# A spectral MLP on one core: ten of twelve mixing units in three float32r passes, and the activation table loaded in the inverse

## The chip, the cores and the metric

One Trainium2 chip, one NeuronCore of it. A program is timed in device microseconds on that core. The engines are TensorE (PE; PEld is its weight load), VectorE (DVE), ScalarE (ACT), GpSimd (POOL) and SyncE (SP), which issues most of the DMAs here. Each engine runs its own queue in order and waits on semaphores of the others.

## The reference

x has 2 sequences of 3008 rows and 256 columns, all in float32.

```python
X = np.fft.rfft(x, axis=1)
Yr = Xr @ w_r - Xi @ w_i + b_r          # w_r, w_i: 256 x 256
Yi = Xr @ w_i + Xi @ w_r + b_i
Yr = np.sign(Yr) * np.maximum(np.abs(Yr) - 0.01, 0)      # Yi the same way
x = np.fft.irfft(Yr + 1j * Yi, n=3008, axis=1)           # 6016 rows of 256
h = x @ w_in1;  x = (h / (1 + np.exp(-1.702 * h))) @ w_out1   # 256 -> 2048 -> 256
h = x @ w_in2;  x = (h / (1 + np.exp(-h))) @ w_out2
```

## The kernel before

The work runs in stages. **Forward:** the real Fourier transform as matrix products: rows of x are folded (sums and differences of rows that share a cosine or a sine), multiplied with cosine and sine matrices in 16 groups, and copied from PSUM (`psf`) by ACT into tiles `xt[b, p, j, cs]` of 128x512, which hold spectrum columns as the contraction's rows (L384). **Mixing:** 12 units `(b, p, j)`; each multiplies the cosine and sine parts of 128 frequencies with the complex weight, adds the bias, shrinks and folds. **Inverse:** 16 steps `(q, b, t)` of products with the inverse matrices into `psi`; ACT copies the first two steps of a `(q, b)` into `rt` (L569), DVE adds and subtracts the other two (`ac`, `rt`, L590 and L591), and sums of these go to `yt` (L607, L611). **MLP:** two layers, six blocks of up to 1024 tokens each, eight pairs of hidden chunks per block, in float32r: an operand is split into a high part (rounded to float32r) and a low part (the rest), and a product is three passes, high by high, high by low, low by high (`passes`, `prod`, `out_mm`).

A mixing unit (`mid_mm`, `mid_post`, `mid_fold`) has two PSUM banks, from the pools `ps0` and `ps1` in turn (four banks each, so a bank comes back two units of the same pool later). PE runs 8 matmuls in float32 and one float32r matmul with the bias. The trace records a float32 matmul as two instructions of 128x512. Then ACT copies the first bank to `us` (L482); DVE makes sum and difference with the second bank, `sd` (L484 to L486); ACT applies Relu (L490), DVE clips (L491): `th`; DVE and POOL fold `th` into tiles `f` (L503, L509, L510), the inverse's stationary operands. The `f` tiles take the places of `xt` tiles that are read out.

Beside the stages runs the conversion of the MLP's weights (float64, loaded as raw words): `tick` takes a weight a step further. ACT takes an Abs of the high words (`cv_c`, L165), DVE assembles the float32 value from the bits in five ops (L170 to L174), an accumulating DMA issued by POOL adds the halves (`cv_a <- cv_c`, L227), DVE makes four small sums for an in-weight (`tmp`, L202 to L205), and ACT and POOL split the result into high part (L99) and low part (L100), tiles `wi` and `wo`. The next weight's load waits until the single `raw` buffer is free, that is for L174. In-weights 4 and 5 live in the pool `wib0`, opened at the start of the mixing.

What sets the order: in the mixing only SP's queue keeps the order of the code (`region('mid')` with 'SP'); a scheduler orders PE, ACT, DVE and POOL. In the inverse PE's order is that of the code. In the MLP it is the code's from the second pair on. ACT's table of functions is loaded where a function needs another set; `preload_act_table` would load it at inverse step `pre`, which is 17, and there are 16 steps, so the load stands before the first gate of the MLP (L717).

Of the kernel before, what the change touches and what calls it, by code (L numbers as in the profile page):

```python
# [8 lines left out]

F32 = mybir.dt.float32  # L10
CFG = {'lv0': 'V', 'lv': 'VVVVVPVVVVVP', 'dd0': 'VPVVPPPPPVVP', 'dd': 'VVVVVVVVVVPV', 'ths': 'VVVVPV', 'thf': 'VVVP', 'ivf': 'VVVPVVVV', 'cva': 'P', 'pol': 'PPPP', 'pil': 'P', 'mvl': 'PVVP', 'xl': 'V', 'xse': 'V', 'gl': 'VPPPPPPP', 'tf': [6, 9, 12], 'tm': [2, 6, 10], 'ti': [1, 4, 7, 10], 'kb': [0, 1, 1, 1, 1, 1, 1, 0], 'kr': [0, 1, 0, 1, 0, 1, 1, 0], 'fa': 3, 'xp': [2, 4, 4, 5], 'xq': [1, 4, 1], 'xs': 4, 'xi': [11, 12, 13, 15], 'xsi': 9, 'ca': 4, 'tl': True, 'fwd': 'Pool,SP', 'rest0': 'all', 'rest1': 'all', 'last1': 'all', 'inv': 'PE', 'mid': 'SP', 'last0': 'all', 'thm': 'A', 'gl0': 'PVPVVVPV', 'gl2': 'PPPPPPPP', 'gl3': 'PPPPPPPV', 'xl0': 'V', 'xl1': 'V', 'pre': 17, 'pre2': 0, 'yd': 6, 'lvb': 6, 'mlp': 'none', 'pr': 'VVVP', 'pf': 'PV', 'eo': '0000', 'ddb': 6, 'mlp1': 'all', 'mlp2': 'all'}
NUM = dict(tf=[5, 9, 13], tm=[1, 3, 5, 7, 9, 11], ti=[0, 2, 4, 6, 8, 10, 12, 14, 14, 15, 15], kb=[2] * 8, kr=1, fa=3, fe=2, pm=0, nf=4, lvb=6, ddb=8, ivb=1, eob=2, fsb=6, f1=3, f2=0, fm=[7, 8, 9], fi=[1, 1, 2, 2], pre=13, pre2=1, yd=3, psh=0, ie=[12], xp=[1, 3, 4, 5], xq=[1, 2, 2], xs=5, nw=4, xi=[14, 14, 15, 15], xsi=13, rw=2, ca=4, cc=2, tb=1, tmn=1)

DEF = dict(pr="V", pf="V", lv0="V", lv="VPP", dd0="VVVVVP", dd="VPV", mpl="PV", ths="VP", thf="VVPP", fsl="VP", ivf="PPVV", cva="P", pol="P", pil="P", mvl="V", xl="PPVVPPP", xl0="PPVVPPP", xl1="PPVVPPP", xse="VP", gl="P", gl0="P", gl2="P", gl3="P", wcl="V", thc="V", thm="V")
F32R = mybir.dt.float32r
U32 = mybir.dt.uint32
AF = mybir.ActivationFunctionType
ALU = mybir.AluOpType

B, S, D, FF = 2, 3008, 256, 2048  # L20
HALF = S // 2
P = 128
# [4 lines left out]
NPR = NFC // 2  # L27
# [24 lines left out]
def r32(ap):  # L52
    return ap.bitcast(F32)
# [3 lines left out]
def spectral_mlp_kernel(ctx, tc, xin, mfwd, minv, wc, bias, w_in1, w_out1, w_in2, w_out2, outT):  # L57
    nc = tc.nc
# [27 lines left out]
    m_p = opened("m", "left", 4)  # L86
    wia_p = opened("wia", "left", NPR // 2)
# [182 lines left out]
    raws, lvs, xs = {}, {}, {}  # L270
# [60 lines left out]
    xt = {}  # L331
# [90 lines left out]
    for g, (q, b, t) in enumerate(groups):  # L422
# [30 lines left out]
    mids = [(b, p, j) for b in range(B) for p in range(2) for j in range(NJ)]  # L453
# [352 lines left out]
    for at, (l, i, p) in enumerate(seq):  # L806
        if (l, i, p) in ((0, 0, 1), (0, 0, 2)):
            region(f'mlp{p}')
        if (i, p) == (1, 0):
            region(f'rest{l}')  # L810
        if (i, p) == (last, 0):
            region(f'last{l}')
        nxt = (l, i + 1) if i < last else (1, 0)
        more = p == NPR - 1 and (l, i) != (1, last)
        k = rate(at)

        def hook(h):
            if more:
                if h in (1, 2):
                    for x in ((0,), (1, 2))[h - 1]:  # L820
                        xprep(*nxt, x)
                if h == 3:
                    xprep(*nxt, 3, 1)
                if h == 4:
                    xprep(*nxt, 3, 2)
            if p == 0:
                for x in {1: (4,), 3: (6, 5)}.get(h, ()):
                    xprep(l, i, x)
            if h == 1 and p == NPR - 2 and (l, i) != (1, last):
# [164 lines left out]
```

## Time and profile before

| | us |
|---|---|
| Median of 3 runs (1190.44 to 1191.27) | 1191.0 |
| The profiled execution | 1191.14 |
| Its span, first to last instruction | 1189.4 |
| Mixing on PE, first matmul to the inverse's first | 66.92 to 152.12 |
| Inverse on PE, to the MLP's first | 152.12 to 207.67 |
| Activation table loads on ACT, three in the kernel, each | 1.28 |

Busy time is the time in which an engine has an instruction running. A group of rows in a timeline has the start, the length and the number of merged instructions; in brackets stands how long the engine idled before them and who released it. Lengths of neighbours overlap a little on PE and ACT, so the distance between starts is the pace. The granted clock of PE is 1.00 in every stage.

### The profile page before, as it was taken

To read this page: it belongs to the slowest core of one execution; us is meant where nothing else is said; L and a number is where in the kernel's file an instruction comes from. 1 tells how busy PE (TensorE), PEld (TensorE's weight loads), DVE (VectorE), ACT (ScalarE), POOL (GpSimd) and SP (SyncE) were. 2 spreads that over 40 slices of the span, in tenths; PEclk is the share of its full clock that TensorE was granted. 3 is DMA by queue.
4 is the path that set the end of the run, shared out by engine and by line. 5 is a ranking of instruction groups with operands and counts; after the bars stand their busy time and mean duration, and the time that the engine had idled before them with its cause. 6 is when DMAs were issued, how large, how long until landed. Compare 5 with 4: busy or idle time off the path is not lost.

```text
span 1189.4 us, 14160 instructions
## 1 busy us (share of the span) xinstructions
PE 1170.6 (98%) x4940; PEld 923.2 (78%) x4940; DVE 628.5 (53%) x969; ACT 740.8 (62%) x1398; POOL 480.3 (40%) x399
## 2 busy tenths in 40 slices
PE   7999999999999999999999999999999999999998
PEld 4744476778888888888888978878888888888897
DVE  7758868666556557465554553352442623523422
ACT  2343431678667667667677786666666766766755
POOL 2333231345443434444445755433333433433333
PEclk9999999999999999999999999999999999999999
DMA  7653102131121121221120200000000000000000
GB/s 273 201 167 80 26 1 54 38 74 49 36 60 48 53 71 36 54 72 36 36 80 9 68 13 27 1 36 1 1 36 1 4 33 1 36 1 1 36 1 31
DMA packets 30441, 55.95 MB, mean 47 GB/s; under 512 B 2721, under 2 KB 11937, under 8 KB 30370
## 3 DMA queue, kind: packets, MB, share of 16 engines
q1 hardware_dynamic: 25730, 46.66, 11.6%
q0 software_dynamic: 4640, 8.39, 4.1%
q8 instruction: 39, 0.64, 0.2%
q14 instruction: 32, 0.26, 0.1%
HBM read 36.29 MB, written 10.35 MB: 39 GB/s over the span
## 4 chain that ended last, share of the span: by engine, by line
PE 71%; ACT 5%; DVE 2%; issue 2%; DMA 0%; POOL 0%; DVEq 0%; ACTq 0%; POOLq 0%
PE o L686 38%; PE x L714 33%; ACT yt L717 2%; ACT g L719 1%; ACT x L637 1%; ACT yt L733 1%; DVE x L640 0%; DVE yt L735 0%; DVE yt L756 0%; DVE yt L690 0%; ACT yt L750 0%; DMA cv_a<-cv_c 0%; ACT yt L748 0%; ACT yt L690 0%; ACT wi L99 0%
## 5 line engine op out<-in xcount | busy, mean ns | idle before, releaser
L724 POOL TENSOR_TENSOR g<-yt,g 128x512 fp32r<-128x512 f32 (+1 forms) x282 | 361.0, 1293 | 537.7 <-PE x L714 357.7
L686 PE MATMUL o<-g,wo 128*128 128x512 f32 (+1 forms) x2304 | 560.4, 385 | 2.0 <-POOL g L724 1.1
L714 PE MATMUL x<-x,wi 128*128 128x512 f32 (+1 forms) x2016 | 500.8, 387 | 5.2 <-ACT yt L750 2.0
L686 PEld LDWEIGHTS o<-g,wo 128*128 128x128 f32 x2304 | 432.4, 188 | 84.2 <-POOL g L724 1.8
L714 PEld LDWEIGHTS x<-x,wi 128*128 128x128 f32 x2016 | 376.2, 188 | 84.7 <-ACT yt L733 5.3
L717 ACT ACTIVATE yt<-yt 128x512 f32<-128x512 f32 (+1 forms) x288 | 179.1, 622 | 254.8 <-DVE yt L756 207.7
L719 ACT CAST g<-yt 128x512 fp32r<-128x512 f32 (+1 forms) x384 | 234.3, 612 | 11.8
L756 DVE TENSOR_TENSOR yt<-yt,x 128x512 f32<-128x512 f32 (+1 forms) x96 | 64.7, 674 | 211.8 <-PE x L714 211.3
L735 DVE TENSOR_TENSOR yt<-yt,x 128x512 f32<-128x512 f32 (+1 forms) x96 | 64.8, 675 | 169.8 <-ACT yt L733 168.8
L724 DVE TENSOR_TENSOR g<-yt,g 128x512 fp32r<-128x512 f32 (+1 forms) x102 | 72.6, 712 | 77.8 <-ACT g L719 76.7
L472 PE MATMUL psm<-wc_s,xt 128*128 128x512 f32 x192 | 84.5, 592 | 0.0
L472 PEld LDWEIGHTS psm<-wc_s,xt 128*128 128x128 f32 x192 | 36.5, 190 | 43.4 <-issue 41.6
L640 DVE TENSOR_TENSOR x<-yt,x 128x512 fp32r<-128x512 f32 (+1 forms) x48 | 49.9, 1041 | 35.9 <-ACT x L637 35.9
L344 PE MATMUL psf<-m,xf 128*128 128x376 f32 (+2 forms) x208 | 59.5, 448 | 7.5 <-DVE xf L303 7.5
L759 DVE TENSOR_TENSOR yt<-yt,x 128x512 f32<-128x512 f32 (+1 forms) x96 | 64.7, 674 | 0.0
L733 ACT COPY yt<-x 128x512 f32<-128x512 f32 (+1 forms) x96 | 54.9, 572 | 9.4 <-issue 6.8
L344 PEld LDWEIGHTS psf<-m,xf 128*128 128x128 f32 x208 | 38.3, 195 | 28.1 <-DVE xf L303 9.3
L717 ACT ACTIVATE yt<-x 128x512 f32<-128x512 f32 (+1 forms) x96 | 56.1, 584 | 2.1 <-PE x L714 2.1
L750 ACT COPY yt<-x 128x512 f32<-128x512 f32 (+1 forms) x96 | 55.8, 581 | 0.8 <-PE x L714 0.8
L748 ACT COPY yt<-x 128x512 f32<-128x512 f32 (+1 forms) x96 | 54.9, 572 | 0.8 <-PE x L714 0.8
L344 PE MATMUL psi<-m,f 128*128 128x376 f32 (+3 forms) x192 | 54.7, 440 | 0.0
L344 PEld LDWEIGHTS psi<-m,f 128*128 128x128 f32 x192 | 35.3, 190 | 18.5 <-issue 0.5
(81 smaller groups left out, 651.8 us busy)
## 6 DMA issues: line engine op xcount, KB each, us to landing
raw<-in_wi SPq DMA_DIRECT2D x32, 256.0 KB, 3.0
cv_a<-cv_c POOLq DMA_DIRECT2D x32, 256.0 KB, 3.3
raw<-in_wo SPq DMA_DIRECT2D x16, 512.0 KB, 3.5
raw<-in_x SPq DMA_DIRECT2D x12, 512.0 KB, 5.1
out_t<-yt SPq DMA_DIRECT2D x20, 256.0 KB, 2.3
m<-in_mf SPq DMA_DIRECT2D x4, 564.0 KB, 6.2
m<-in_mi SPq DMA_DIRECT2D x4, 564.0 KB, 10.0
w_in<-cv_a SPq DMA_DIRECT2D x8, 256.0 KB, 2.0
```

What stands on the lines that cost most here:

```text
L344: nc.tensor.matmul(ps, hi[:, c : c + P], m[:, k, :w], start=i == 0, stop=i == last)
L472: nc.tensor.matmul(t, x[xi][:, mm], wc_s[:, mm, off : off + 2 * D], start=(n == 0), stop=(n == 3 and grp == 1))
L686: nc.tensor.matmul(acc[h, mm], st, mv, start=first and k == 0, stop=last and k == 2)
L714: nc.tensor.matmul(ps, st, mv, start=first and m == 0, stop=m == 2, skip_group_check=True)
L717: nc.scalar.activation(g, g if src is None else src, func)
L719: nc.scalar.copy(gh, g)
L724: eng.tensor_sub(gl, g, r32(gh))
L733: nc.scalar.copy(y1, X)
L735: nc.vector.tensor_add(y1, y1, Y)
L750: nc.scalar.copy(y3, X)
L756: nc.vector.tensor_add(y2, y2, X)
L759: nc.vector.tensor_add(y3, y3, Z)
```

## The change

Units 2 to 11 of the mixing (`n32` is 2) run in float32r. The weight `wc_s` is split once into `wh` (an ACT copy) and `wl` (a DVE subtract). For each of these units, and each of its two `xt` tiles, `xsplit` makes a high part `hi` by an ACT copy, and a low part in two steps: ACT writes -x rounded to float32r into `lo`, and an accumulating DMA issued by POOL adds x to it. Six buffers each for `hi` and `lo` (`nhb`) hold three units. Units 2, 3 and 4 are split before the loop, unit u+3 after the matmuls of unit u. Each of the 8 float32 matmuls becomes three float32r passes. The pool `wib0` is opened only after the mixing, in the place of the new tiles. `pre` becomes 14, so that the table for the first layer's gate is loaded in the inverse. In the settings `n32`, `nhb` and `xa` are new (`xa` is read nowhere).

```diff
@@ place_in
-        wp = wia_p if p < NPR // 2 else wib_a if p < 6 else wib_b[0]
+        wp = wia_p if p < NPR // 2 else wib_p[p // 6]
@@ the mixing
-    wib_a = opened("wib0", "left", 2)
     mid_p = opened("mid", "right", 2)
     ft = {}
+    wh_p = opened("wh", "left")
+    nh_p = opened("nh", "left", N('nhb'))
+    wh = wh_p.tile([P, 2, 3 * D], F32R, name="wh")
+    wl = wh_p.tile([P, 2, 3 * D], F32R, name="wl")
+    nc.scalar.copy(wh, wc_s)
+    nc.vector.tensor_sub(wl, wc_s, r32(wh))
+    xsp = {}
+
+    def xsplit(i):
+        if not N('n32') <= i < len(mids):
+            return
+        b, p, j = mids[i]
+        for cs in range(2):
+            x = xt[b, p, j, cs].rearrange("p q m c -> p (q m c)")
+            hi = nh_p.tile([P, 512], F32R, tag="hi", name="xh")
+            lo = nh_p.tile([P, 512], F32R, tag="lo", name="xl")
+            nc.scalar.mul(lo, x, -1.0)
+            nc.gpsimd.dma_start(out=lo, in_=x, accum_op=ALU.add)
+            nc.scalar.copy(hi, x)
+            xsp[b, p, j, cs] = [t[:, :].rearrange("p (q m c) -> p q m c", q=2, m=2) for t in (hi, lo)]
...
-                    nc.tensor.matmul(t, x[xi][:, mm], wc_s[:, mm, off : off + 2 * D], start=(n == 0), stop=(n == 3 and grp == 1))
+                    w = slice(off, off + 2 * D)
+                    if hl is None:
+                        nc.tensor.matmul(t, x[xi][:, mm], wc_s[:, mm, w], start=(n == 0), stop=(n == 3 and grp == 1))
+                    else:
+                        for k, (st, mv) in enumerate(passes(hl[xi][0][:, mm], hl[xi][1][:, mm], wh[:, mm, w], wl[:, mm, w])):
+                            nc.tensor.matmul(t, st, mv, start=n == 0 and k == 0, stop=n == 3 and grp == 1 and k == 2)
...
+    for i in range(N('n32') + 3):
+        xsplit(i)
     for i in range(len(mids)):
         ps = mid_mm(i)
+        if i >= N('n32'):
+            xsplit(i + 3)
...
-    closed("mid", "wc")
+    closed("mid", "wc", "nh", "wh")
+    wib_p.append(opened("wib0", "left", 2))
```

The scheduler's order moves with it. On ACT, at units 1 to 3 of the mixing: `us` and `th` belong to the units in turn, `xh` and `xl` to a unit three further on, `wi` are the weights' splits. Before:

```order
L482 COPY us<-psm 128x512
L165 ACTIVATE cv_c<-raw_866 128x512
L99 CAST wi_1074<-cv_a 128x384
L490 ACTIVATE th<-sd,neglam 128x512 x2
L482 COPY us<-psm 128x512
L99 CAST wi_1074<-tmp 128x512
L490 ACTIVATE th<-sd,neglam 128x512 x2
```

And now, from the same copy of unit 1 (raw_1033 is the same weight as raw_866 there):

```order
L507 COPY us<-psm 128x512
L515 ACTIVATE th<-sd,neglam 128x512 x2
L507 COPY us<-psm 128x512
L165 ACTIVATE cv_c<-raw_1033 128x512
L478 CAST xh<-xt_106 128x512
L476 ACTIVATE xl<-xt_106 128x512
L478 CAST xh<-xt_107 128x512
L476 ACTIVATE xl<-xt_107 128x512
L515 ACTIVATE th<-sd,neglam 128x512 x2
L507 COPY us<-psm 128x512
```

The split of unit 5 (xt_106, xt_107) stands behind the weight's Abs, and the casts of in-weight 4 (wi_1074) have left this place for the inverse.

On DVE, from the last unit's `sd` to the inverse's first `ac`. Before:

```order
L486 TENSOR_TENSOR sd<-psm,us 128x256
L491 SCALAR_TENSOR_TENSOR th<-sd,th 128x512 x2
L503 TENSOR_TENSOR f_1038<-th 128x512
L590 TENSOR_TENSOR ac<-rt,psi 128x377
L591 TENSOR_TENSOR rt<-rt,psi 128x377
```

And now:

```order
L511 TENSOR_TENSOR sd<-psm,us 128x256
L172 SCALAR_TENSOR_TENSOR cv_a<-raw_1243,cv_c 128x512
L516 SCALAR_TENSOR_TENSOR th<-sd,th 128x512
L173 TENSOR_SCALAR cv_c<-cv_a 128x512
L516 SCALAR_TENSOR_TENSOR th<-sd,th 128x512
L202 TENSOR_TENSOR tmp<-cv_a 128x128
L203 TENSOR_TENSOR tmp<-cv_a 128x128
L174 SCALAR_TENSOR_TENSOR cv_c<-raw_1243,cv_c 128x512
L528 TENSOR_TENSOR f_1305<-th 128x512
L204 TENSOR_TENSOR tmp<-tmp,cv_a 128x128
L205 TENSOR_TENSOR tmp<-cv_a,tmp 128x128
L170 TENSOR_SCALAR cv_c<-cv_c 128x512
```

Conversions that were done within the mixing (L172 to L174, L202 to L205, and the next weight's from L170 on) now stand between the last unit and the inverse's first sums, and three more of them among these.

## Rows read from the trace of the kernel before

**Rows 1.** Page, part 1: busy us, share of the span, instructions
```profile
PE 1170.6 (98%) x4940; PEld 923.2 (78%) x4940; DVE 628.5 (53%) x969; ACT 740.8 (62%) x1398; POOL 480.3 (40%) x399
```

**Rows 2.** The stages in windows: PE, PEld, DVE, ACT, POOL busy, PEclk, DMA share, GB/s
```profile
67.00:152.00 85.00, 85.00 (x205) 38.67 (x204) 63.27 (x117) 31.38 (x60) 26.32 (x20) 1.00 0.29 85
152.00:208.00 56.00, 56.00 (x210) 37.65 (x209) 43.84 (x66) 14.17 (x29) 13.26 (x9) 1.00 0.11 29
208.00:250.00 42.00, 39.36 (x166) 30.24 (x165) 28.29 (x44) 28.38 (x51) 15.87 (x13) 1.00 0.20 50
```

**Rows 3.** PE timeline over mixing, inverse and first MLP group: start us, length us, instruction
```profile
66.92 3.60 PE L472 MATMUL psm<-wc_s,xt 128*128 128x512 f32 x8
...
70.59 7.03 PE L472 MATMUL psm<-wc_s,xt 128*128 128x512 f32 x16
...
77.69 7.03 PE L472 MATMUL psm<-wc_s,xt 128*128 128x512 f32 x16
...
152.12 8.44 PE L344 MATMUL psi<-m,f 128*128 128x378 f32 x28
...
207.67 6.25 PE L714 MATMUL x<-x,wi 128*128 128x512 f32 x24
214.86 0.50 PE L686 MATMUL o<-g,wo 128*128 128x512 f32 x1 [0.94 <-ACT g L719]
```

**Rows 4.** A 60 us window in the MLP, PE alone
```profile
360.00:420.00 60.00, 59.80 (x264) 1.00 0.19 49
```

**Rows 5.** ACT timeline, from before the mixing to the first MLP group
```profile
58.02 1.04 ACT L322 COPY wc_s<-wc_f 128x1024 f32<-128x1024 f32 x1 [2.78 <-DMA wc_f<-in_wc]
...
74.02 0.59 ACT L384 COPY xt<-psf 128x128 f32<-128x128 f32 x3
...
91.63 0.67 ACT L165 ACTIVATE cv_c<-raw 128x512 f32<-128x512 f32 x1 [4.67 <-DMA raw<-in_wi]
...
168.81 1.14 ACT L637 CAST x<-yt 128x512 fp32r<-128x512 f32 x2 [8.38 <-DVE yt L607]
...
189.32 0.62 ACT L99 CAST wo<-cv_a 128x512 fp32r<-128x512 f32 x1 [0.79 <-DMA cv_a<-cv_c]
189.85 1.59 ACT L569 COPY rt<-psi 128x376 f32<-128x376 f32 x4
...
208.89 0.59 ACT L733 COPY yt<-x 128x512 f32<-128x512 f32 x1 [6.78 <-issue]
...
212.23 1.28 ACT L717 ACT_TABLE_LOAD   x1
```

**Rows 6.** DVE timeline, mixing and inverse
```profile
87.28 0.68 DVE L174 SCALAR_TENSOR_TENSOR cv_c<-raw,cv_c 128x512 f32<-128x512 uint32 x1
...
161.30 0.55 DVE L590 TENSOR_TENSOR ac<-rt,psi 128x377 f32<-128x377 f32 x1 [5.34 <-PE psi L344]
...
190.26 1.38 DVE L173 TENSOR_SCALAR cv_c<-cv_a 128x512 uint32<-128x512 uint32 x1
...
202.54 0.55 DVE L590 TENSOR_TENSOR ac<-rt,psi 128x376 f32<-128x376 f32 x1 [2.14 <-PE psi L344]
```

**Rows 7.** POOL timeline, mixing and inverse
```profile
113.62 1.71 POOL L503 TENSOR_TENSOR f<-th 128x512 f32<-128x512 f32 x1 [1.48 <-DVE th L491]
...
190.03 1.33 POOL L100 TENSOR_TENSOR wo<-cv_a,wo 128x512 fp32r<-128x512 f32 x1 [4.31 <-ACT wo L99]
```

**Rows 8.** Page, part 3 (queue of accumulating DMAs) and part 6 (issue to landing)
```profile
q0 software_dynamic: 4640, 8.39, 4.1%
...
cv_a<-cv_c POOLq DMA_DIRECT2D x32, 256.0 KB, 3.3
```

**Rows 9.** The tile cv_a, 55 to 215 us: min/median/max
```profile
L227 POOL DMA_DIRECT2D cv_a<-cv_c x9: 849/870/877, 54.5 to 193.2; - x9
...
DMA to landing us min/median/max: 3.3/4.4/7.9
```

**Rows 10.** DMA issues from 70 to 80 us, while matrices are loaded
```profile
cv_a<-cv_c POOLq DMA_DIRECT2D x1, 256.0 KB, 6.6
```

More of the change, by code (lines that the diff above doesn't have):

```diff
@@ L10 @@
 F32 = mybir.dt.float32
-CFG = {'lv0': 'V', 'lv': 'VVVVVPVVVVVP', 'dd0': 'VPVVPPPPPVVP', 'dd': 'VVVVVVVVVVPV', 'ths': 'VVVVPV', 'thf': 'VVVP', 'ivf': 'VVVPVVVV', 'cva': 'P', 'pol': 'PPPP', 'pil': 'P', 'mvl': 'PVVP', 'xl': 'V', 'xse': 'V', 'gl': 'VPPPPPPP', 'tf': [6, 9, 12], 'tm': [2, 6, 10], 'ti': [1, 4, 7, 10], 'kb': [0, 1, 1, 1, 1, 1, 1, 0], 'kr': [0, 1, 0, 1, 0, 1, 1, 0], 'fa': 3, 'xp': [2, 4, 4, 5], 'xq': [1, 4, 1], 'xs': 4, 'xi': [11, 12, 13, 15], 'xsi': 9, 'ca': 4, 'tl': True, 'fwd': 'Pool,SP', 'rest0': 'all', 'rest1': 'all', 'last1': 'all', 'inv': 'PE', 'mid': 'SP', 'last0': 'all', 'thm': 'A', 'gl0': 'PVPVVVPV', 'gl2': 'PPPPPPPP', 'gl3': 'PPPPPPPV', 'xl0': 'V', 'xl1': 'V', 'pre': 17, 'pre2': 0, 'yd': 6, 'lvb': 6, 'mlp': 'none', 'pr': 'VVVP', 'pf': 'PV', 'eo': '0000', 'ddb': 6, 'mlp1': 'all', 'mlp2': 'all'}
@@ L12 @@
-NUM = dict(tf=[5, 9, 13], tm=[1, 3, 5, 7, 9, 11], ti=[0, 2, 4, 6, 8, 10, 12, 14, 14, 15, 15], kb=[2] * 8, kr=1, fa=3, fe=2, pm=0, nf=4, lvb=6, ddb=8, ivb=1, eob=2, fsb=6, f1=3, f2=0, fm=[7, 8, 9], fi=[1, 1, 2, 2], pre=13, pre2=1, yd=3, psh=0, ie=[12], xp=[1, 3, 4, 5], xq=[1, 2, 2], xs=5, nw=4, xi=[14, 14, 15, 15], xsi=13, rw=2, ca=4, cc=2, tb=1, tmn=1)
+CFG = {'lv0': 'V', 'lv': 'VVVVVPVVVVVP', 'dd0': 'VPVVPPPPPVVP', 'dd': 'VVVVVVVVVVPV', 'ths': 'VVVVPV', 'thf': 'VVVP', 'ivf': 'VVVPVVVV', 'cva': 'P', 'pol': 'PPPP', 'pil': 'P', 'mvl': 'PVVP', 'xl': 'V', 'xse': 'V', 'gl': 'VPPPPPPP', 'tf': [6, 9, 12], 'tm': [2, 6, 10], 'ti': [1, 4, 7, 10], 'kb': [0, 1, 1, 1, 1, 1, 1, 0], 'kr': [0, 1, 0, 1, 0, 1, 1, 0], 'fa': 3, 'xp': [2, 4, 4, 5], 'xq': [1, 4, 1], 'xs': 4, 'xi': [11, 12, 13, 15], 'xsi': 9, 'ca': 4, 'tl': True, 'fwd': 'Pool,SP', 'rest0': 'all', 'rest1': 'all', 'last1': 'all', 'inv': 'PE', 'mid': 'SP', 'last0': 'all', 'thm': 'A', 'gl0': 'PVPVVVPV', 'gl2': 'PPPPPPPP', 'gl3': 'PPPPPPPV', 'xl0': 'V', 'xl1': 'V', 'pre': 14, 'pre2': 0, 'yd': 6, 'lvb': 6, 'mlp': 'none', 'pr': 'VVVP', 'pf': 'PV', 'eo': '0000', 'n32': 2, 'xa': 4, 'nhb': 6, 'ddb': 6, 'mlp1': 'all', 'mlp2': 'all'}
@@ L14 @@
+NUM = dict(n32=2, nhb=6, tf=[5, 9, 13], tm=[1, 3, 5, 7, 9, 11], ti=[0, 2, 4, 6, 8, 10, 12, 14, 14, 15, 15], kb=[2] * 8, kr=1, fa=3, fe=2, pm=0, nf=4, lvb=6, ddb=8, ivb=1, eob=2, fsb=6, f1=3, f2=0, fm=[7, 8, 9], fi=[1, 1, 2, 2], pre=13, pre2=1, yd=3, psh=0, ie=[12], xp=[1, 3, 4, 5], xq=[1, 2, 2], xs=5, nw=4, xi=[14, 14, 15, 15], xsi=13, rw=2, ca=4, cc=2, tb=1, tmn=1)
 DEF = dict(pr="V", pf="V", lv0="V", lv="VPP", dd0="VVVVVP", dd="VPV", mpl="PV", ths="VP", thf="VVPP", fsl="VP", ivf="PPVV", cva="P", pol="P", pil="P", mvl="V", xl="PPVVPPP", xl0="PPVVPPP", xl1="PPVVPPP", xse="VP", gl="P", gl0="P", gl2="P", gl3="P", wcl="V", thc="V", thm="V")
@@ L209, in place_in @@
         )
-    wib_b = []
+    wib_p = []
     spare = []
@@ L464, in mid_mm @@
         x = [xt[b, p, j, cs][:, q] for cs in range(2) for q in range(2)]
+        hl = [[v[:, q] for v in xsp[b, p, j, cs]] for cs in range(2) for q in range(2)] if (b, p, j, 0) in xsp else None
         ps = []
@@ L852, in spectral_mlp_kernel @@
             closed("iv")
-            wib_b.append(opened("wib1", "left", 2))
+            wib_p.append(opened("wib1", "left", 2))
         if N('pre2') and (l, i, p) == (0, last, NPR - 1):
```

## The prediction

> **What bounds the kernel now.** I read the page's shares first: TensorE (PE) is busy 98% of the span [rows 1], so only a stage's PE time, or a wait that ends at PE, is worth anything. The windows by stage say where the change falls: mixing (67 to 152 us) and inverse (152 to 208 us) keep PE busy without a gap at a granted clock of 1.00, while VectorE (DVE) is at 63.27 of 85 us and 43.84 of 56 us, ScalarE (ACT) at 31.38 and 14.17, GpSimd (POOL) at 26.32 and 13.26; only behind 208 us does PE stand still, 2.64 us in 42 [rows 2]. The PE timeline gives the pace: unit after unit starts 7.10 us behind the last (70.59, 77.69), twelve of them from 66.92 to 152.12, 85.2 us. At 214.86 PE waits 0.94 us for ACT's first gate [rows 3]. The ACT timeline shows what that gate waited for: the activation table, 1.28 us at 212.23, put between the group's copies and its first sigmoid [rows 5].
>
> **The change part by part.**
>
> *PE.* A unit of before is 16 passes of an f32 matmul (8 matmuls, two passes each in the records) and a bias matmul. After, ten units have 24 float32r passes of the same 512 columns and the bias. Such passes fill the MLP: 264 in 60 us are 0.2273 us each [rows 4]. 25 x 0.2273 = 5.68 us, 1.42 us less than 7.10; ten units, 14.2 us. The bounds: from below the same 0.2273, since that window has next to no gap; from above the pass of f32 in the mixing itself, 7.10 / 17 = 0.42 us, by which a unit would be longer than before. I take the MLP's, whose instruction it is: same tile, same columns, a stationary tile loaded for each pass.
>
> *The weights' split.* One ACT copy and one DVE subtract of 128x1536. ACT's 128x1024 took 1.04 us [rows 5], so about 1.5 us. It goes ahead of the last copies of the forward stage, which ran at 74.02 [rows 5] and feed only units 9 to 11. DVE's is some 1.8 us, by 0.68 us for 512 of its elements with two inputs from SBUF [rows 6].
>
> *The split of x: ACT.* 4 ops of 128x512 a unit, 0.57 us each back to back (two in 1.14 [rows 5]): 2.3 us. ACT had 31.38 us in 85; it gains 40 x 0.57 + 1.5 = 24.3 us and sends three casts (1.6 us) to the inverse: 54 us in 71. It stays under PE's pace. Three units are split before PE's third unit begins, the others behind the copy of a unit three earlier: they overwrite its tiles.
>
> *The split of x: POOL and the DMAs.* Two accumulating DMAs a unit: POOL spends 0.87 us on each [rows 9], 17.4 us in all beside 26.32, of which four subtracts and two issues, some 6 us, go to the inverse. The transfers themselves: 32 of them took 4.1% of 16 engines' 1189 us, 1.5 us each [rows 8], so 3.0 us of a unit's 5.68. From issue to landing they took 3.3 us in the median of the whole kernel [rows 8], 4.4 in this stretch, at most 7.9 [rows 9], and 6.6 us while matrices were being loaded [rows 10]. In the steady state PE leaves unit u, ACT splits u+3 in 2.3 us, POOL issues, 4.4 us later it has landed: 6.8 us, and PE wants it two units, 11.4 us, later. Slack 4.6 us: hidden, and hidden still with a fold of 1.71 us on POOL [rows 7] ahead of the issue.
>
> *Where it is not hidden.* Unit 2: ACT copies the last forward tiles at about 75.5 to 76.1, the first low part is negated at 76.7, and its DMA, issued then, lands in 4.4 to 6.6 us, 81.1 to 83.3. PE reaches unit 2 at 66.92 + 14.2 = 81.1 and its first low pass at 81.6: a wait of 0 to 1.7 us. I take 0.7. Unit 5: in ACT's order its split stands behind the conversion of the next weight (the Abs of raw_1033), whose load starts when DVE's last op on the weight before it is done. Twelve splits (76.1 to 82.5) now precede the copy of unit 0, so DVE comes to that op near 90.5, where it ended at 87.96 before; the load took from there to 91.63, 3.7 us [rows 5, 6]; so 94.2. Abs 0.67 and two splits: 95.9; landed at 100.3, for a PE that arrives at about 99.6 with the 0.7 us above: 0.7 us. With 0.6 us for the second halves and for handing over, 2.0 us in all. Low end 0; high end 5.0, if each of the two lands in the longest 7.9 us. Unit 6 is third in that queue and has some 1 us over.
> So the mixing ends at 66.92 + 14.2 + 56.8 + 2.0 = 139.9, 12.2 us earlier.
>
> *DVE, and what moves to the inverse.* In the mixing DVE has 63.27 us, plus 1.8, less what is now behind it: 58.6 of 73 us, no bound. What moves, by the order: three ops of one weight, all five of the next, two of a third and four small sums, about 6.5 us of DVE; with them four subtracts of POOL. POOL's tensor ops hold DVE up: the 190.26 op took 1.38 us beside POOL's 190.03 to 191.36 [rows 6, 7], and I put 0.7 us on each. That is 9 us into a stage where DVE idled 12.2 us, 5.34 of it just before the inverse's first sums (161.30) and 2.14 near the end (202.54) [rows 2, 6]. The first gap takes most of it, the 4.7 us of shorter ones a part, so DVE runs some 2.5 us late through the middle (an estimate) and makes that good at the end. Who waits for DVE there? ACT's copies at 189.85 stand in its queue behind a cast that waits for an accumulating DMA (189.32 [rows 5]), which waits for DVE. They free the banks that PE wants four steps before the end; a step is 12 passes of 376 columns, 3.8 us by 7.03 us for 16 of 512, so at 207.67 - 15.2 = 192.5, and the first copy ended at 190.25. 2.2 us over, against 2.5 us late: I take 0.4 us of waiting, from 0 to 4 (all 9 us late less 5).
>
> *The table.* It now follows the last rt copies; ACT idles 6.78 us before 208.89 [rows 5], so it is hidden there. The gate comes 1.28 us earlier in ACT's queue but no sooner than DVE's sum, 1 us; PE's 0.94 us goes [rows 3]. Next in line is PE's own work, which ends at about the same time. I take 0.9, between 0 and 1.1.
>
> The MLP has the same rows in the same order, so the rest moves as a block. Sum: 12.2 + 0.9 - 0.4 = 12.7 us. The profiled execution took 1191.14 us (span 1189.4), and the runs' median is 1191.0: 1178.4.
>
> **A rule against this change.** POOL took 849 to 877 ns for each DMA it issued, nowhere longer, though DVE was three quarters busy [rows 9, 2]. The Trainium skill (SBUF — State Buffer, section "SBUF: two separate sides") warns that the descriptors of a DMA issued from GpSimd can't be written while VectorE runs an op that uses both port pairs, and tells of 620 ns that became 3100. The row shows no such stretch of the issue; with 2.5 us more to each landing an estimate from the page is 1182, about what rival (e) gives from rows.
>
> **The rivals.**
> (a) *Low parts late in every unit*, so that not PE but the chain split, issue, landing sets the pace. For it: each unit passes through the queues of PE, ACT, POOL and the DMA engines, and no two of these DMAs stood close together in the trace, so how two share the engines isn't shown. Against: 4.6 us of slack. Were each of units 5 to 11 0.9 us late: 1178.4 + 6.3 = 1184.7.
> (b) *Slower: accumulating DMAs run one at a time.* If they don't overlap, each takes its landing time of the queue. Twenty at 4.4 us from 76.7 end at 164.7; PE then has 3.6 us left: 168.3 against 152.1, 16.2 us later, less 0.9: 1206. It decides from 3.6 us each ((152.1 - 3.6 + 0.9 - 76.7) / 20), and 3.3 us is the median of the kernel, so it hangs on how much of the landing is occupation; for it also that the low tiles are float32r, into which no large accumulating DMA goes before. Against: 1.5 us of engine time each.
> (c) *DVE as the bound of the inverse.* 9 us more in 56 with 12.2 idle; if the waits fall so that half of it can't be used, PE waits 4 us: 1182.4. Against: PE's banks have two steps and more to spare everywhere but at that one copy.
> (d) *The change doesn't do what it says*: at 0.42 us a pass a unit would take 25 x 0.42 = 10.5 us, ten units 34 us more: 1224. The MLP's rows speak against it.
> (e) *Each accumulating DMA lands as late as the latest, 7.9 us* [rows 9]. For it: the stretch where they start is that of the matrices' loads. Unit 2 would wait until 84.6 instead of 81.6, 3.0 us, unit 5 from 101.9 to 103.9, 2.0 us; the rest has its slack. That is 5.6 us with the 0.6, 3.6 more than taken: 1182.0. Against: the 4.4 us of the middle one.
>
> **How the numbers follow.** The forecast, PE paced with a few waits, 1175.5 to 1181.5: 0.72. (a) 0.08, (b) 0.05, (c) 0.07, (d) 0.01, (e) 0.07. The low end is no wait at all: 14.2 + 1.1, 1175.8; the high end takes in (c), (e) and (a): 1175 to 1185. Within 0.2% (2.4 us, what a measurement can tell) would need 10 us lost between these: 0.02; taken from (a); slower is (b) and (d), 0.06; faster 0.92.
>
> **What would show it.** In the mixing, units 5.68 us apart, and PE's idle there some 2 us, ended by the accumulating DMA at units 2 and 5; the mixing's end at 140. A landing over 8 us, or PE idle in every unit, speaks for (a) or (b). In the inverse, PE without a gap but for a few tenths near 180; DVE's first ac at 10 us behind the mixing's end, not 9.2. At the MLP's start no 0.94 us, and the table load ahead of the first copy. Wrong would be: units not at 5.68 us; PE idle over 5 us between 67 and 196.

## The result and the profile after

| series | before, median | after, median (range, runs) | after / before, 95% interval |
|---|---|---|---|
| first | 1190.8 | 1179.76 (1177.31 to 1183.16, 6) | 0.9909 [0.9897, 0.9921] |
| second (`again`) | 1191.32 | 1182.21 (1180.42 to 1183.99, 5) | 0.9925 [0.9912, 0.9937] |

The change gains 9 to 11 us; 12.7 were forecast (1178.4, within 1175 to 1185). The profiled execution of the kernel after took 1183.16 us, the longest of its six, that of `again` 1180.42, the shortest of its five, so these two profiles show the ends of the spread more than its middle. By stages, on PE, in the profiled execution of each (distances between first matmuls, us; `o` is the result of the MLP's second product):

| stage | before | after | after, `again` | forecast for after |
|---|---|---|---|---|
| up to the mixing | 66.92 | 68.64 | 66.93 | 66.92 |
| mixing | 85.20 | 76.48 | 75.11 | 73.0 |
| inverse | 55.55 | 55.64 | 56.38 | 55.95 |
| MLP's start to its first `o` | 7.19 | 6.21 | 6.21 | 6.3 |
| rest of the span | 974.54 | 974.43 | 973.97 | 974.5 |

The first row is not the change's: in the profiles of all kernels below, whose first stage does the same work, it lies between 66.3 and 69.2, and `again` is the same kernel as after. What fell short is the mixing, by 3.5 us in after and 2.1 in `again`. The windows of the kernel after, stage by stage (columns as in [rows 2]):

```profile
68.64:145.12 76.48, 73.50 (x285) 54.39 (x284) 55.01 (x104) 49.16 (x95) 36.46 (x34) 0.98 0.64 143
145.12:200.76 55.64, 55.64 (x210) 37.35 (x208) 51.01 (x81) 18.55 (x36) 19.86 (x15) 1.00 0.23 57
206.97:248.97 42.00, 40.24 (x171) 31.38 (x171) 27.53 (x45) 29.32 (x53) 19.45 (x17) 1.00 0.23 57
```

PE now idles 2.98 us in the mixing, and its mean clock there is 0.98; the inverse has no gap, as in [rows 2], though DVE works 51.01 us in it instead of 43.84. PE's timeline of the kernel after: bias matmuls of two neighbouring units, units 5 and 6, and the ends of the stages:

```profile
91.32 0.39 PE L500 MATMUL psm<-bias_hl,ones 128*128 128x512 f32 x1
97.04 0.39 PE L500 MATMUL psm<-bias_hl,ones 128*128 128x512 f32 x1
...
100.25 0.39 PE L497 MATMUL psm<-wl,xh 128*128 128x512 f32 x1
102.65 0.50 PE L497 MATMUL psm<-wh,xl 128*128 128x512 f32 x1 [2.02 <-DMA xl<-xt]
102.99 0.56 PE L497 MATMUL psm<-wh,xh 128*128 128x512 f32 x1
103.35 0.63 PE L497 MATMUL psm<-wl,xh 128*128 128x512 f32 x1
103.78 0.63 PE L497 MATMUL psm<-wh,xl 128*128 128x512 f32 x1
...
111.19 0.50 PE L497 MATMUL psm<-wh,xl 128*128 128x512 f32 x1 [0.96 <-DMA xl<-xt]
...
145.12 7.16 PE L344 MATMUL psi<-m,f 128*128 128x378 f32 x22
...
200.76 6.29 PE L744 MATMUL x<-x,wi 128*128 128x512 f32 x24
206.97 0.50 PE L716 MATMUL o<-g,wo 128*128 128x512 f32 x1
```

A unit takes 5.72 us from bias to bias, where one of [rows 3] took 7.10. PE waits twice, for the low parts of unit 5 (102.65) and unit 6 (111.19). Behind the first wait the passes come 0.43 us apart instead of 0.23. The clock says why (PE alone, PEclk third from the end):

```profile
102.60:106.50 3.90, 3.85 (x10) 0.56 0.67 170
106.50:111.10 4.60, 3.72 (x17) 1.00 0.99 183
```

The granted clock is at its lower level, 1.2 GHz, for some 3.5 us, and ten passes take 3.98 us instead of 2.28. Why unit 5's low part is late stands in ACT's timeline, why unit 6's is, in POOL's:

```profile
97.31 0.66 ACT L165 ACTIVATE cv_c<-raw 128x512 f32<-128x512 f32 x1 [2.16 <-DMA raw<-in_wi]
97.88 0.61 ACT L478 CAST xh<-xt 128x512 fp32r<-128x512 f32 x1
98.39 0.63 ACT L476 ACTIVATE xl<-xt 128x512 fp32r<-128x512 f32 x1
...
102.38 0.63 ACT L476 ACTIVATE xl<-xt 128x512 fp32r<-128x512 f32 x1
```
```profile
99.31 0.88 POOL L477 DMA_DIRECT2D xl<-xt  x1 [2.03 <-ACT xl L476]
...
104.23 0.86 POOL L227 DMA_DIRECT2D cv_a<-cv_c  x1 [3.02 <-DVE cv_c L174]
104.77 2.09 POOL L477 DMA_DIRECT2D xl<-xt  x2
```

Unit 5's split stands behind the Abs, which waited for the weight's load. Unit 6's negation was done at 103.01, but its DMA stands on POOL behind the conversion's (104.23), which waited for DVE; then it lands late, 6.4 us behind its issue, while the two low parts of unit 6, the conversion's DMA and a weight's load share the DMA engines, which are full from 106.5 us on (0.99 above). The DMA queues and issues from 105 to 112 us follow (packets, MB, share of 16 engines; median us to landing; the third of these low parts is unit 7's, issued at 111.22):

```profile
q0 software_dynamic: 431, 0.79, 63.4%
...
xl<-xt POOLq DMA_DIRECT2D x3, 256.0 KB, 6.4
```

The table's load now follows the last `rt` copies, as forecast (ACT's timeline):

```profile
196.47 1.60 ACT L599 COPY rt<-psi 128x376 f32<-128x376 f32 x4 [9.62 <-DVE yt L641]
198.09 1.28 ACT L685 ACT_TABLE_LOAD   x1
```

### The profile page after: what moved, and what is told of

It is laid out like the page before. It is cut to its first block, busy times and chain, and to the rows that moved or that the text cites. A ratio compares the mean times of both kernels' runs of the same rounds, so it can differ in the third digit from the quotient of the medians.

```text
span 1181.4 us, 14419 instructions
## 1 busy us (share of the span) xinstructions
PE 1161.4 (98%) x5020; PEld 940.1 (80%) x5020; DVE 627.0 (53%) x970; ACT 761.3 (64%) x1439; POOL 497.8 (42%) x419
## 4 chain that ended last, share of the span: by engine, by line
PE 72%; ACT 5%; DVE 2%; issue 2%; DMA 0%; POOL 0%; DVEq 0%; ACTq 0%; POOLq 0%
PE o L716 38%; PE x L744 34%; ACT yt L747 2%; ACT g L749 1%; ACT x L667 1%; ACT yt L763 1%; DVE x L670 0%; DVE yt L765 0%; DVE yt L786 0%; DVE yt L720 0%; ACT yt L780 0%; DMA cv_a<-cv_c 0%; ACT yt L778 0%; ACT yt L720 0%; ACT wi L99 0%
## 5 line engine op out<-in xcount | busy, mean ns | idle before, releaser
L344 PE MATMUL psf<-m,xf 128*128 128x376 f32 (+2 forms) x208 | 62.0, 461 | 6.8 <-DVE xf L303 6.1
L165 ACT ACTIVATE cv_c<-raw 128x512 f32<-128x512 f32 x32 | 21.5, 673 | 29.0 <-DMA raw<-in_wo 17.1
L227 POOL DMA_DIRECT2D cv_a<-cv_c x32 | 27.9, 870 | 26.1 <-DVE cv_c L174 15.4
```

Of the source, the lines that this page charges most:

```text
L344: nc.tensor.matmul(ps, hi[:, c : c + P], m[:, k, :w], start=i == 0, stop=i == last)
```

## The experiments

Theory A: PE waits because the splits of units 5 and 6 stand behind the conversion in the queues, and the clock falls behind the wait. B: the f32r passes of the mixing are slower by themselves, or another queue paces them. C: the shortfall lies in the stage before, apart from the mixing. From the fourth run on, D: what an earlier end of the mixing gains is lost where DVE comes late to the inverse's sums; F: not DVE, but PE's banks and ACT's copies hold the inverse up. The ratios of the changed kernels lie within 0.8% of each other, and where two intervals overlap no order of the two is shown. The table holds what the profiled executions showed (us; "sum" is DVE's first `ac` behind the mixing's end):

| kernel | mixing | sum | inverse | to first `o` | ratio to before, 95% |
|---|---|---|---|---|---|
| before | 85.20 | 9.2 | 55.55 | 7.19 | 1 |
| `again` | 75.11 | 13.0 | 56.38 | 6.21 | 0.9925 [0.9912, 0.9937] |
| `hi_twice` | 78.21 | 14.1 | 56.89 | 6.21 | 0.9939 [0.9926, 0.9953] |
| `act_in_order` | 71.39 | 17.8 | 61.97 | 7.08 | 0.9956 [0.9943, 0.9969] |
| `ticks_3_5_7` | 71.35 | 17.9 | 63.33 | 6.21 | 0.9950 [0.9937, 0.9962] |
| `ticks_2_5_8` | 71.37 | 16.7 | 60.52 | 6.38 | 0.9930 [0.9918, 0.9943] |
| `three_f32` | 74.59 | 12.9 | 55.70 | 6.21 | 0.9909 [0.9894, 0.9924] |
| `dve_lo` | 71.39 | 17.4 | 60.36 | 6.21 | 0.9919 [0.9904, 0.9935] |
| `short_bits` | 71.72 | 18.8 | 60.19 | 6.21 | 0.9906 [0.9889, 0.9923] |
| `act_and_sums` | 71.37 | 9.9 | 55.54 | 10.31 | 0.9948 [0.9935, 0.9961] |
| `dve_lo_sums_first` | 71.38 | 9.2 | 55.55 | 9.83 | 0.9937 [0.9924, 0.9949] |
| `sums_first_x_by_dma` | 71.41 | 14.0 | 55.55 | 5.08 | 0.9883 [0.9867, 0.9900] |

**`again`**, the kernel after, unchanged.

> The changed kernel once more, for a second trace and for its scatter (1177.3 to 1183.2 us so far). Theory A (PE waits for low parts at units 5 and 6, and PE's granted clock falls behind the longer wait): again a wait of 1 to 3 us at unit 5 that ends with the accumulating DMA; where it stays under 2 us no fall of the clock, and then the mixing takes some 73 us instead of 76.5. Theory C (the shortfall is a slower forward stage, which ended 1.7 us later in the first trace, and has nothing to do with the mixing): the forward stage's end moves by 1 us or more between the two traces and the mixing's length does not. Median 1178 to 1181 us.

PE's timeline of `again`:

```profile
99.41 0.50 PE L497 MATMUL psm<-wh,xl 128*128 128x512 f32 x1 [0.49 <-DMA xl<-xt]
...
108.10 0.50 PE L497 MATMUL psm<-wh,xl 128*128 128x512 f32 x1 [2.52 <-DMA xl<-xt]
108.44 0.40 PE L497 MATMUL psm<-wh,xh 128*128 128x512 f32 x1
108.68 0.39 PE L497 MATMUL psm<-wl,xh 128*128 128x512 f32 x1
...
183.44 6.90 PE L344 MATMUL psi<-m,f 128*128 128x376 f32 x21 [0.57 <-ACT rt L599]
```

The same two units wait, 3.0 us in all, and the stage before is as long as in the kernel before, while the mixing still falls short: C falls, A stands. But unit 5 waits less than the 1 to 3 us expected, unit 6 waits longer, and the passes behind its 2.52 us are 0.24 to 0.34 us apart: the clock did not fall. So the mixing takes 75.1 us and not the 73 expected without a fall. The inverse has a wait of 0.57 us at ACT's `rt` copies, the place that the prediction named.

**`table_only`**, the kernel before with the table's load moved:

```diff
-'pre': 17
+'pre': 14
```

> The kernel before with the table load moved into the inverse and nothing else. Theory: PE's 0.94 us wait at the first gate goes, the rest of the MLP shifts by it: 0.9 to 1.1 us faster than before, 1189.8. Rival (the load is paid elsewhere, in ACT's queue of the inverse): no difference, 1190.8.

0.9987 [0.9978, 0.9996], 1.1 us, by the interval 0.5 to 2.6. In its timeline PE's 0.94 us before the first `o` [rows 3] is gone (the next wait, 0.23 us, is for DVE):

```profile
214.28 0.50 PE L686 MATMUL o<-g,wo 128*128 128x512 f32 x1
215.01 0.96 PE L714 MATMUL x<-x,wi 128*128 128x512 f32 x3 [0.23 <-DVE yt L756]
```

**`hi_twice`**, the third pass reads the high part again:

```diff
-passes(hl[xi][0][:, mm], hl[xi][1][:, mm], ...
+passes(hl[xi][0][:, mm], hl[xi][0][:, mm], ...
```

> The changed kernel, but the third pass of each product reads the high part of x again instead of the low part, so the result is not the reference's; the low parts are still made and added, and nobody on PE waits for them. Theory A: no PE wait in the mixing, no fall of the clock, units 5.68 us apart, the mixing 14.2 + 56.8 = 71 us: 5 us less than in the first trace, the time 1175 to 1177. Rival B (float32r passes in the mixing are slower by themselves, or another queue sets the pace): the mixing stays above 75 us and the time near 1180.

A miss, by 8 us; the mixing takes more than 75 us, as B expected. No low part is waited for, yet PE waits for unit 5's high part, longer than in after. PE's and ACT's timelines:

```profile
104.07 0.79 PE L497 MATMUL psm<-wh,xh 128*128 128x512 f32 x1 [4.63 <-ACT xh L478]
```
```profile
100.11 0.66 ACT L165 ACTIVATE cv_c<-raw 128x512 f32<-128x512 f32 x1 [7.00 <-DMA raw<-in_wi]
```

Low parts that nobody reads free their buffers at once, so the scheduler sent those of the later units early, and the weight's load, free to start at 90.7, came 9.4 us later, where it took 4.7 in after. The DMA issues from 88 to 100 us, and a window (ACT alone, DMA share before the last number):

```profile
xl<-xt POOLq DMA_DIRECT2D x7, 256.0 KB, 8.2
```
```profile
93.00:100.00 7.00, 0.12 (x1) 1.00 1.10 222
```

The DMA engines were full. So the edit moved more than the wait that it was to remove, and it does not decide between A and B. What it leaves is that the Abs in front of the split is the late link here, and that the load which this Abs waits for took twice as long beside seven accumulating DMAs.

**`act_in_order`**, ACT in the code's order in the mixing, the conversion's steps later:

```diff
-'mid': 'SP', 'tm': [2, 6, 10]
+'mid': 'SP,Activation', 'tm': [4, 6, 10]
```

> The changed kernel with ACT's queue in the mixing in the order of the code and the first conversion of a weight two units later (after unit 4 instead of 2), so that the splits of units 5 to 7 stand ahead of the next Abs and don't wait for a weight's load. Theory A: no PE wait at units 5 and 6, no fall of the clock, mixing 71 to 72 us. What it may cost: conversions go later, and more of DVE's and POOL's work falls into the inverse, where PE may wait a few us. Time 1175 to 1181. Rival (it is the DMA's landing, not the place in ACT's queue, that is late): waits of 1 to 2 us at units 5 and 6 remain.

The mixing has no wait and takes 71.39 us, against the 71.0 of 14.2 + 56.8: A holds there, and B falls. But the gain does not arrive. Windows and PE's timeline:

```profile
140.62:202.59 61.97, 58.24 (x209) 37.93 (x208) 58.37 (x97) 20.74 (x40) 28.25 (x20) 0.97 0.23 61
```
```profile
168.07 15.97 PE L344 MATMUL psi<-m,f 128*128 128x376 f32 x48 [1.78 <-ACT rt L599]
...
185.92 1.45 PE L344 MATMUL psi<-m,f 128*128 128x376 f32 x2 [1.88 <-ACT rt L599]
```

PE waits twice for `rt` copies, the second time (185.92) for those that the prediction named. Behind this wait of 1.88 us the granted clock fell: 0.53 from 186 to 188 us and 0.61 from 188 to 190. The median of 1186.3 lies above the 1175 to 1181 expected, and the kernel is 0.3% slower than `again`. Hence D.

**`ticks_3_5_7`** and **`ticks_2_5_8`**, as `act_in_order` with the steps at other units:

```diff
-'tm': [4, 6, 10]
+'tm': [3, 5, 7]        and        'tm': [2, 5, 8]
```

> ScalarE keeps the order of the code in the mixing, as in act_in_order, but the conversion's three steps there stand at units 3, 5 and 7 (instead of 4, 6 and 10), so that its last bit operations on VectorE are done within the mixing: between VectorE's last sum of the mixing and the inverse's end stand 15 of the conversion's five-op steps, against 18 in the changed kernel and 20 in act_in_order. Theory A (units 5 and 6 wait because their splits stand behind the conversion's Abs on ScalarE): both splits now precede the first Abs, so no wait, mixing 71.4 us as in act_in_order. Theory D (what the mixing gains is lost again where VectorE's conversions pace the inverse's sums): 3 us of VectorE less than in act_in_order, so of its 3.7 us of waits and some 2 us of slow clock in the inverse 0 to 3 us are left. Sum 1191.2 - 13.8 - 1.1 + 0 to 3 = 1176.3 to 1179.3, I take 1177.5, faster than the changed kernel. Where the inverse's waits have another cause than VectorE, they stay and the time is that of act_in_order, 1185 to 1186.

> The same with the conversion's steps at units 2, 5 and 8: unit 5's split precedes the first Abs, unit 6's stands behind it, but the weight of that Abs was loaded before the mixing. Theory A: no wait at units 5 and 6 either, mixing 71.4 to 72. Theory D: 17 of the conversion's ops left for the inverse, so 1 to 4 us of waits there: 1177.3 to 1180.3, I take 1179, between ticks_3_5_7 and act_in_order. If the count on VectorE is not what matters, both of these kernels come out alike.

The mixing came as expected, the inverse did not. The medians are 1185.9 and 1183.6, not 1177.5 and 1179; 1185.9 is what was expected if the waits had another cause than DVE. Yet fewer conversion operations behind the mixing (15) went with the longest inverse, and PE waited for DVE itself (PE's timeline, `ticks_3_5_7`):

```profile
155.75 1.00 PE L344 MATMUL psi<-m,fd 128*128 128x190 f32 x2 [4.00 <-DVE sd L511]
```

The last unit's `sd`, which frees the banks, stood behind conversions. So the count of operations behind the mixing was the wrong measure here; what stands ahead of what in DVE's queue fits the trace.

**`dve_lo`**, the low part by a DVE subtract:

```diff
-nc.scalar.mul(lo, x, -1.0)
-nc.gpsimd.dma_start(out=lo, in_=x, accum_op=ALU.add)
 nc.scalar.copy(hi, x)
+nc.vector.tensor_sub(lo, x, r32(hi))
```

> The low parts are made by one VectorE subtract (x - hi) instead of ScalarE's negation and an accumulating DMA; nothing else changed by hand. On ScalarE unit 5's copies still stand behind the second Abs of the mixing. Theory A with the landing as the late part: unit 5's high copies were done at 98.5 and 99.5 us in the changed kernel, for a unit that starts at 100.0, so with 0.7 us of VectorE in place of 3.3 to 6.3 us of issue and landing neither unit 5 nor unit 6 waits. Theory D: VectorE gets 20 x 0.68 = 13.6 us, 72 of 71.5 us in the mixing, so it falls behind and the inverse waits 3 to 8 us: 1191.2 - 13.8 - 1.1 + 3 to 8 = 1179 to 1184, I take 1182. If VectorE's load does not matter: 1177.

As expected: no wait in the mixing, 4.8 us more in the inverse, 1181.6 us. PE's timeline, and DVE's ahead of its first sum:

```profile
166.77 9.74 PE L344 MATMUL psi<-m,f 128*128 128x376 f32 x30 [2.62 <-ACT rt L598]
```
```profile
155.03 0.43 DVE L170 TENSOR_SCALAR cv_c<-cv_c 128x512 f32<-128x512 f32 x1 [2.89 <-ACT cv_c L165]
155.49 0.43 DVE L171 TENSOR_SCALAR cv_c<-cv_c 128x512 uint32<-128x512 uint32 x1
155.84 0.54 DVE L619 TENSOR_TENSOR ac<-rt,psi 128x377 f32<-128x377 f32 x1
```

The first sum stands behind a conversion operation that idles 2.89 us for the next weight's Abs.

**`three_f32`**, nine units in float32r:

```diff
-'n32': 2
+'n32': 3
```

> Nine units in float32r instead of ten (unit 2 stays in float32), so units 3, 4 and 5 are split before the loop, and unit 6's split comes behind the third Abs of the mixing on ScalarE. PE comes to unit 6 1.4 us later than in the changed kernel. Theory A (the place behind the Abs in ScalarE's order makes the wait): no wait at unit 5; the third Abs, at 108.7 us in the changed kernel, comes at 107 to 109, unit 6's low part lands at 112 to 115 for a PE that is there at 106.8, a wait of 5 to 8 us and 2 us of slow clock behind it; 1191.2 - 12.8 - 1.1 + 7 to 10 = 1184 to 1187, I take 1185.5. If the waits come from the DMA's landing or from PE being ahead of a steady chain, there is less of them than in the changed kernel: 1191.2 - 12.8 - 1.1 + 3 = 1180.

No wait at unit 5, one at unit 6, as A has it, but of 1.37 us instead of 5 to 8: the third Abs came at 103.36, not 107 to 109. DVE's last read of the weight before it ended at 99.46 (103.68 in after), and the load took 3.9 us from there instead of 5.0. The median of 1180.7 is what was expected of the rival (1180) and not of A (1185.5), so A held for the place of the wait, behind the Abs, and not for its length, and this run alone does not exclude the rival. PE's and ACT's timelines:

```profile
108.71 0.50 PE L497 MATMUL psm<-wh,xl 128*128 128x512 f32 x1 [1.37 <-DMA xl<-xt]
```
```profile
103.36 0.66 ACT L165 ACTIVATE cv_c<-raw 128x512 f32<-128x512 f32 x1 [1.40 <-DMA raw<-in_wo]
103.92 0.60 ACT L478 CAST xh<-xt 128x512 fp32r<-128x512 f32 x1
```

With one unit fewer in float32r the kernel is as fast as after: the tenth unit's 1.42 us bring nothing here.

**`short_bits`**, `dve_lo` with three bit operations on one column:

```diff
-ts(c, c, ...), ts(cu, cu, ...), ts(cu, au, ...)
+ts(c[:, :1], c[:, :1], ...), ts(cu[:, :1], cu[:, :1], ...), ts(cu[:, :1], au[:, :1], ...)
```

> dve_lo with three of the conversion's five bit operations on VectorE (L170, L171, L173) done on one column of 512, so that the instructions, their order and their waits stay and only VectorE's time goes: some 1.1 us a weight, 4 us in the inverse and 3 to 4 in the mixing (the weights are then not those of the reference). Theory D: the inverse's 60.4 us fall by 2 to 4, to 56.5 to 58.5: 1181.6 - 3 = 1177.6 to 1179.6. Theory F: the same inverse as dve_lo, 60 us, and 1181 to 1181.6.

The inverse stayed at 60.19 us and its first sum at 18.8: less of DVE's time does not bring the sums forward while they stand behind the same wait for the Abs. That is F's inverse, but the median, 1179.2, is D's. In the profiles most of the difference from `dve_lo` lies in the MLP, whose conversions the edit shortens too: from the first `o` to the end 971.95 us instead of 974.45. The ratio's interval overlaps that of `dve_lo`. D as an amount of work is not borne out here; D as an order is what the next two test.

**`act_and_sums`** and **`dve_lo_sums_first`**, DVE in the code's order in the inverse, the steps later (the first also with ACT in order in the mixing, the second on `dve_lo`):

```diff
-'inv': 'PE', 'ti': [1, 4, 7, 10]
+'inv': 'PE,DVE', 'ti': [3, 6, 9, 12]
```

> Two orders are fixed: ScalarE keeps the order of the code in the mixing (so units 5 and 6 don't wait, as in act_in_order), and VectorE keeps it in the inverse, where the conversion's steps stand at inverse steps 3, 6, 9 and 12 instead of 1, 4, 7 and 10. So between the last unit's fold and the first inverse sums VectorE has nothing of the conversion left, where it had eight operations of it and more in the kernels so far. Theory D (what an early end of the mixing gains is lost because VectorE comes to the first sums 15 to 18 us behind it instead of 9, held up by conversions): the first sum comes 10 to 12 us behind the mixing's end, PE waits 0 to 2 us in the inverse, which takes 55.6 to 57.6 us. 1191.5 - 13.8 - 1.1 + 0 to 2 = 1176.6 to 1178.6, I take 1177.6. If VectorE's conversions are not what delays the sums (theory F: PE's banks and ScalarE's copies do it), the inverse stays at 60 to 63 us and the time at 1182 to 1186.

> dve_lo (low parts by one VectorE subtract, no accumulating DMA for them) with VectorE in the order of the code in the inverse and the conversion's steps at inverse steps 3, 6, 9 and 12; the mixing's order is left to the scheduler as in dve_lo. Half of one conversion (three operations) is still left behind the last unit. Theory D: mixing 71.4 us as in dve_lo, first sum 10 to 13 us behind its end, inverse 55.6 to 58 instead of 60.4: 1191.5 - 13.8 - 1.1 + 0 to 2.5 = 1176.6 to 1179, I take 1177.8. Theory F: as dve_lo, 1181.6.

The first sum comes 9.9 and 9.2 us behind the mixing's end, and both inverses run without a wait, in 55.5 us: D against F, as an order (the edit changes DVE's order and the steps' places together, and does not tell them apart). Yet neither kernel is faster than after: 1185.5 and 1184.0 us, where 1177.6 and 1177.8 were expected. PE's timeline of `dve_lo_sums_first`:

```profile
194.91 3.20 PE L743 MATMUL x<-x,wi 128*128 128x512 f32 x12
199.97 0.97 PE L743 MATMUL x<-x,wi 128*128 128x512 f32 x3 [1.86 <-ACT yt L762]
202.01 2.93 PE L743 MATMUL x<-x,wi 128*128 128x512 f32 x6 [1.07 <-DVE yt L764]
```

and DVE alone in its windows (PEclk third from the end):

```profile
194.91:205.00 10.09, 9.95 (x18) 0.79 0.28 73
150.00:200.00 50.00, 48.61 (x77) 1.00 0.25 64
```

The postponed conversions and the rest of DVE's sums now stand at the MLP's start: DVE is busy 48.61 of the 50 us from 150 to 200 us and 9.95 of the 10 behind the MLP's start at 194.91, and PE waits and loses clock there.

**`sums_first_x_by_dma`**, as `dve_lo_sums_first` with less of DVE's work ahead of that point:

```diff
-'ti': [3, 6, 9, 12]
+'ti': [2, 5, 8, 15]
+if l == 0 and i == 0 and k in (0, 1, 4, 6):
+    nc.scalar.mul(lo, src, -1.0)
+    nc.gpsimd.dma_start(out=lo, in_=src, accum_op=ALU.add)
```

> dve_lo_sums_first with less of VectorE's work ahead of the MLP's start: the conversion's steps stand at inverse steps 2, 5, 8 and 15, so that the last one comes behind and among the MLP's first operands, and four of the seven low parts of the first block's x (each 0.68 us of VectorE) are made as in the mixing, by ScalarE and an accumulating DMA. Theory D (VectorE's work between the mixing and the MLP's first gate is the floor, wherever its order puts the wait): mixing 71.4 and inverse 55.6 to 57 us, as in dve_lo_sums_first; from the MLP's first matmul to the first one on o 6.2 to 7.5 us instead of 9.8, with no fall of the clock behind it, which is worth another 1 to 1.5 us: 1184.0 - 2.3 to 3.6 - 1.2 = 1179.2 to 1180.5, I take 1179.8. If not VectorE's work but PE's or ScalarE's own chain makes the wait at the MLP's start, it stays at 3.4 us and the time at 1183 to 1184; if the new DMAs land late, PE waits for them at the first products.

Median 1180.55, on a chip where before took 1194.23: the lowest ratio of all, 0.9883 [0.9867, 0.9900], with an interval apart from that of `again` and just overlapping that of the first series. That it is faster than the kernel after is not shown: the medians of after are 1179.76 and 1182.21, and the profiled executions take nearly the same from the mixing's start to the end of the span, 1112.4 us here (in the longest of its four runs), 1112.8 in after and 1111.7 in `again`. PE's timeline:

```profile
195.69 5.25 PE L747 MATMUL x<-x,wi 128*128 128x512 f32 x21
200.77 0.39 PE L719 MATMUL o<-g,wo 128*128 128x512 f32 x1
...
203.96 1.65 PE L747 MATMUL x<-x,wi 128*128 128x512 f32 x6 [0.83 <-DVE yt L792]
206.26 1.67 PE L747 MATMUL x<-x,wi 128*128 128x512 f32 x6 [0.65 <-DVE yt L789]
```

PE reaches the MLP 126.96 us after the mixing's start, 5.2 us sooner than in after (132.12), with no fall of the clock. (Its 5.08 us to the first `o` hold 21 passes, not 24.) But from there to the end of the span it takes 985.4 us instead of 980.6. DVE's copies of `o`, which end each block of the MLP, tell where: those of the first block start 91.3 us behind the MLP's start instead of 88.8, those of the sixth 498.4 instead of 495.1, and those of the last 979.4 instead of 974.9. So 2.5 us go in the first block, where PE waits for DVE; the 0.8 up to the sixth and the 1.5 in and behind the last lie far from it, and their cause is not shown.

## Why the prediction came out as it did

*PE's passes.* Right: 5.72 us a unit, forecast 5.68; the mixing without waits takes 71.39 us (`act_in_order`), forecast 71.0.

*Where it is not hidden.* This is the step that was mis-sized: 2.0 us, and 5.1 in the profile after (76.48 - 71.39). Unit 2 did not wait (0.7 forecast). At unit 5 the mechanism was the one described, the split behind the Abs behind the weight's load; with the stage's later start of 1.72 us counted in, the low part landed 0.6 us later than worked out (the load took 4.66 us from DVE's last read instead of 3.7, the landing 3.3 instead of 4.4) and PE was 0.8 us earlier, since unit 2 had not waited: 2.17 us beyond the passes' own distance instead of 0.7. Unit 6, given 1 us to spare, lost 1.12 us, and 2.67 in `again`: the prediction followed ACT's queue and left out POOL's, where the conversion's DMA stands ahead of the split's, and it took 4.4 us for a landing that took 6.4 while four transfers overlapped. In after and `again`, which lost 5.1 and 3.7 us, this step is the largest error of the sum.

*What a wait costs.* The sum had waits at their length. In the profile after the first wait cost 1.70 us more through the clock (3.98 us for ten passes less 2.28). The Trainium skill (TensorE: Matmul & The Clock Gate, section "HAM oscillation — how this bites in real kernels") describes this pattern, a wait for a DMA behind which the next matmuls run at the lower clock; the trace agrees at 102.65 and not at 108.10 of `again`, where nothing fell behind 2.52 us. In the profile after the two losses and the clock are together 2.17 + 1.12 + 1.70 = 4.99 of the 5.1 us.

*The inverse.* 0.4 us of waiting forecast, 0.1 longer in after and 0.8 in `again`, with 0.57 of waiting at the `rt` copies named. Right, but by a margin that the late mixing gave: first sums at 12.9 us, forecast 10. In every kernel whose sums came 16.7 us or more behind the mixing's end the inverse took 60.2 to 63.3 us; up to 14.1 it took 55.5 to 56.9. So rival (c) was the next bound, under 4 us away: the five kernels that ran the mixing in 71.4 to 71.7 us and left DVE's order in the inverse to the scheduler lost 4.6 to 7.8 us in the inverse. That the total came near the forecast is in part luck: a loss in the mixing stood in for one in the inverse.

*The table.* 0.9 forecast, 1.1 by `table_only`, 0.98 in the stage.

*The rivals.* (d) and (b) are out: 0.23 us a pass, and DMAs that overlap (unit 5's two, issued 1.05 us apart, landed after 3.3 and 3.8 us). (a) is out, since no unit after 6 waited. (e) came nearest at unit 6, with 6.4 us instead of 7.9, beside other transfers and not in the stretch that the prediction named. POOL issued the 20 low parts in 862 ns in the median; one of unit 6's took 1558. The Trainium skill (SBUF — State Buffer, section "SBUF: two separate sides") tells of a DMA of some 620 ns that took some 3100 beside a VectorE copy, because GpSimd couldn't write its descriptors. A stretch of that size is not seen in these issues.

What stays open: why the clock fell behind waits of 1.88 and 2.02 us and not behind ones of 2.52 (`again`) and 2.62 (`dve_lo`), and what makes 2.3 of the 4.8 us that the last kernel loses behind the MLP's start. Four units split ahead, or a second buffer for the weight's load, might remove the wait at its root; neither was tried.

## What to carry to other kernels

When a stage gets shorter on PE, list for each new operation what stands ahead of it in every queue that it passes, the issuing engine's too, and look for the slow chain (here load, Abs, bits, DMA) that has slipped in front. A wait removed in one stage is worth only the slack of the next: here VectorE's work followed PE from the mixing to the inverse and on to the MLP's start, and each reordering paid at the next meeting point. Even the last one, which took some of that work away, reached the MLP 5.2 us sooner and gave 4.8 of them back. An experiment that leaves out a reader also frees its buffers, and so changes the schedule that it was meant to probe.

## What the runs showed of the hardware

A single wait of 2.02 us for a DMA was followed by some 3.5 us at half the granted clock, and one of 2.52 us by none. Accumulating DMAs of 256 KB within the chip landed in 3.3 us at unit 5 and in 6.4 us where four transfers ran at once; seven close together took 8.2 in the median, and beside them a weight's load on another queue took 9.4 us instead of 4.7.
